# LayerNorm's little tiles allocated in front of the big buffers

## The chip, the cores and the metric

The kernel runs on one core of one Trainium2 chip. The metric is the device time of one execution in microseconds (us): the median of the runs of a kernel.

## The reference

With x of 2048 rows and 512 columns (float32) the kernel computes a gated Fourier mixing layer:

```python
xn  = (x - mean(x)) / sqrt(var(x) + 1e-5)                  # over the 512 columns
a   = xn @ dft_hid_re.T;  b = xn @ dft_hid_im.T
s   = dft_seq_re @ a - dft_seq_im @ b                      # 2048 x 2048 by 2048 x 512
h   = relu(xn @ w1 + b1)                                   # 512 -> 1792
g   = silu((h * h) @ w2 + b2)                              # 1792 -> 512
out = x + s * g
```

## The kernel before

Every float32 operand is kept as a sum of two parts, a high and a low one, of a type that TensorE reads (`F32R`, 4 bytes an element), and each product is three matmuls: high by high, high by low, low by high (`PASSES`). ScalarE makes the high part (L68), VectorE the low one (L71). Many products are made from four blocks with the seven products of Strassen and Winograd (`PRODUCTS`, numbered 1 to 7 in `ORDER`), so that operands stand in tiles of several slots of 256 columns.

A matmul names two operands in the on-chip memory: a stationary one of 128 columns, which a weight load (LDWEIGHTS) brings into the array, and a moving one of 256 or 512 columns, which streams past it. The stages, in the order in which they run:

- **Plain products**, `products` (L330), c = 0 and 1: each is 192 matmuls of 512 columns. Weights: `XC` (xc0 to xc7, the normalised x). Moving: `part`, in g1a and g1b.
- **Products by seven**, `mm` (L277), c = 2 to 7, eight steps j each, so 48 steps of 42 matmuls of 256 columns. Weights: `XC`. Moving: for the products 1, 2 and 3 the buffers g0a and g0b, for 4, 5, 6 and 7 g1a and g1b (`B_SLOT`).
- **Second transform**, `stage2` (L263), 16 times 24 matmuls of 512 columns, laid between the above. Weights: `PQ` (pq00 to pq11). Moving: `WD` (wd0 and wd1).
- **First dense layer**, `hidden` (L517), four chunks c of tokens with seven units p each, 42 matmuls of 256 columns a unit. Weights: `W1[p]`, for p = 0 to 5 in xc2 to xc7, for p = 6 in g0b (slots 0 to 2, 18 matmuls) and g1b (slots 3 to 6, 24 matmuls). Moving: `xT`, in xc0 and xc1 for the even c, in wd0 and wd1 for the odd c (L307).
- **Second dense layer**, `outer` (L571), again four c with seven p of 42 matmuls. Weights: `ready`, in xc4 to xc6. Moving: `W2[p]`, for p = 0 to 4 in xc0, xc1, xc7, xc2 and xc3, for p = 5 and 6 in wd0 and wd1 (`W2_HOME`, L466).

These stages hold 5136 matmuls; 13 more warm TensorE up at the start (L352). The matmuls of a stage stand in one queue in the program's order. Each waits for its operands alone, and the elementwise work and the transfers for the next steps run beside them. The order is written out by hand.

All on-chip buffers are tiles of one pool. A tag's buffer is given its address when the tag is first asked for, one behind the other, each rounded up to 32 bytes. In front stand 1152 bytes of constants and scratch and the small tiles b1s, b2s, eps, stats and stats_t (L81 to L85), up to byte 3552 of a partition. LayerNorm's little tiles are "bn" (48 bytes, three buffers, L117) and "sm" (16 bytes, three buffers, L127). They are first asked for after xc0 to xc7, r, the pq, g0a and g0b have their places, and before g1a, wd0, g1b, wd1, t, e and sx have theirs.

Of the kernel before, what the change touches and what calls it, by code (L numbers as in the profile page):

```python
# [12 lines left out]
P = 128  # L13
# [48 lines left out]
def fnet_gated_kernel(ctx, tc, x, xt, ct, wd, w1, w2, b1, b2, out):  # L62
# [32 lines left out]
    def buf(tag, shape, name, dtype=F32, bufs=1):  # L95
        return pool.tile(shape, dtype, tag=tag, bufs=bufs, name=name)

    def bcast(src, n):
        return bass.AP(tensor=src.tensor, offset=src.offset, ap=[[0, P], [1, n]])

# [13 lines left out]

    def ln_stats(j, hs=slice(0, 2)):
        t = xr[j]
        sm = buf("bn", [P, 12], f"bn{j}_{hs.start}", bufs=3)  # L117
        for h in range(hs.start, hs.stop):
            bn = sm[:, 6 * h:6 * h + 6]
            nc.vector.bn_stats(bn, t[:, h])  # L120
            nc.vector.bn_aggr(stats[:, :, h, j], bn)

    root = {}

    def ln_root(j, hs=slice(0, 2)):
        n = hs.stop - hs.start
        t = root[j] = buf("sm", [P, 4], f"root{j}_{hs.start}", bufs=3)  # L127
        nc.scalar.activation(t[:, 0:n], stats[:, 1, hs, j], AF.Sqrt, bias=eps)

    def ln_rstd(j, hs=slice(0, 2)):  # L130
# [119 lines left out]
    def pq(c, m, dh, src=None):  # L250
        t = PQ[c, m, dh] = buf(f"pq{m}{dh}", [P, 2, 512], f"pq{c}_{m}_{dh}", F32R)
        if src is not None:
            split(t[:, HI], t[:, LO], src)
        return t
# [28 lines left out]
    def load_rows(c, t):  # L283

        flat = rows.rearrange("a b -> (a b)")
        for m in range(2):
            for h in range(2):
                n = m * S + c * TC + h * 256
                nc.sync.dma_start(t[:, 2 * m + 1 - h], bcast(flat[n:n + 256], 256))
        xT["rows"] = t  # L290
# [46 lines left out]
    with tc.manual_schedule(engines=None):  # L337
# [10 lines left out]
        for n, (count, dtype) in enumerate(zip(WARM, (mybir.dt.bfloat16, F32R))):  # L348
            zeros = buf("g0" + "ab"[n], [P, 512], f"zeros{n}", dtype)
            nc.vector.memset(zeros if n == 0 else zeros.bitcast(F32), 0.0)  # L350
            for _ in range(count):
                nc.tensor.matmul(warm, zeros[:, 0:P], zeros, start=True, stop=True)  # L352
        plain_banks(0)
        ln_stats(0, one)
        ln_root(0, one)
        for h, hs in enumerate((one, two)):
            g = plain_parts(0, 0, hs)
            split_hi(*g)
            ln_rstd(0, hs)
            ln_xn(0, h)  # L360
            split_hi(*xc_parts(0, h))
            if h == 0:
                ln_stats(0, two)
                ln_root(0, two)
            split_lo(*g)
            if h == 1:
                ln_stats(1)
                g = plain_parts(0, 1)
                split_hi(*g)
                ln_root(1)  # L370
            split_lo(*xc_parts(0, h))
            products(0, 0, h, True)
        load_c(0, 3)
        load_x(4)
        for j in range(1, NJ):
            ln_rstd(j)
            for h in range(2):
                ln_xn(j, h)
                split_hi(*xc_parts(j, h))
            split_lo(*g)  # L380
            load_c(*order[j + 3])
            if j + 4 < NJ:
                load_x(j + 4)
            split_lo(*xc_parts(j, 0))
            if j + 1 < NJ:
                ln_stats(j + 1)
                ln_root(j + 1)
            xn_lo = split_lo(*xc_parts(j, 1))
            for h in range(2):
                products(0, j, h, j == 1)  # L390
            g = plain_parts(*order[j + 1])
            split_hi(*g)
            if j == 2:
                nc.sync.dma_start(b1s, b1)
                nc.sync.dma_start(b2s, bcast(b2, D))
        split_lo(*g)

    for n, (c, j) in enumerate(order):
# [20 lines left out]
        if j == NJ - 1:  # L419
            for dh in range(2):  # L420
                for m in range(2):
                    t = pq(c, m, dh)
# [216 lines left out]
    for c, j in steps:  # L639
# [21 lines left out]
        if c == NC - 1:  # L661

            if j in (2, 3):
                q = j - 2
                t = buf(f"xc{2 + q}", [P, 3, 4, 256], f"stage{q}")
# [197 lines left out]
def _launch(arrays, out_shape):  # L863
    import numpy as np
    import concourse.bacc as bacc
    from concourse.bass_utils import run_bass_kernel_spmd

    nc = bacc.Bacc("TRN2", target_bir_lowering=False, num_devices=1, dynamic_dma_scratch_size=1024)
    feed, args = {}, []
    for name, v in arrays.items():  # L870
        v = np.ascontiguousarray(v)
        feed[f"in_{name}"] = v
        args.append(nc.dram_tensor(f"in_{name}", v.shape, mybir.dt.from_np(v.dtype), kind="ExternalInput").ap())
    args.append(nc.dram_tensor("out_0", out_shape, F32, kind="ExternalOutput").ap())
    with tile.TileContext(nc, schedule_with_timeline_sim=True) as tc:
        fnet_gated_kernel(tc, *args)
    r = run_bass_kernel_spmd(nc, [feed], core_ids=[0])
    return r.results[0]["out_0"]
# [25 lines left out]
```

## Time and profile before

| | us |
|---|---|
| median of 3 runs (721.21 to 721.50) | 721.28 |
| span of the profiled execution | 719.5 |
| TensorE busy within that span | 706.7 |
| VectorE busy | 584.7 |
| ScalarE busy | 347.6 |

The profile is of one execution. Its span runs from its first to its last instruction; what lies around the span is the 1.8 us by which the median is above it. PE stands for TensorE's matmuls, PEld for its weight loads, DVE for VectorE, ACT for ScalarE. Matmuls follow each other without a gap in most of the span, and each one's recorded duration overlaps the next, so the time that a matmul takes of the span is read from pieces of the chain: the length of a piece by the number of matmuls in it.

### The profile page before, as it was taken

What the parts mean: (1) busy time and instruction counts of PE and PEld (TensorE: products, weight loads), DVE (VectorE), ACT (ScalarE), POOL (GpSimd) and SP (SyncE); (2) the same over time, 40 slices, a digit from 0 to 9 for tenths busy, and PEclk for the clock granted to TensorE, in tenths of its full rate; (3) what the DMA queues carried; (4) which work ended last, traced back from release to release, by engine and by line L of the source; (5) the groups of instructions that cost most, each with busy time, mean ns of one, the idle gap of its engine ahead of it and who ended that gap; (6) DMA issues with size and microseconds to landing.
All of it is one profiled execution on the core that took longest, in us unless ns stands there. A gap on an engine that the chain in (4) does not pass through costs nothing.

```text
span 719.5 us, 12692 instructions
## 1 busy us (share of the span) xinstructions
PE 706.7 (98%) x5149; PEld 665.4 (92%) x5149; DVE 584.7 (81%) x886; ACT 347.6 (48%) x475; POOL 5.2 (1%) x8
## 2 busy tenths in 40 slices
PE   8999999999999999999999999999999999999996
PEld 5778789999999999999998999999999999999996
DVE  7999554679598697797795955999988979989895
ACT  4438233434353544444542424777767764444441
POOL 0000000000000000000000000000000000101000
PEclk9999999999999999999999999999999999999999
DMA  9622540633553653744824669965625995767643
GB/s 325 217 88 89 169 137 16 220 107 128 206 205 132 218 189 122 273 152 139 298 92 147 224 243 337 352 248 205 255 112 188 343 405 196 187 205 199 219 146 111
DMA packets 55018, 141.09 MB, mean 196 GB/s; under 512 B 5040, under 2 KB 21680, under 8 KB 53680
## 3 DMA queue, kind: packets, MB, share of 16 engines
q1 hardware_dynamic: 49840, 124.56, 49.5%
q10 hardware_dynamic: 4032, 14.68, 5.2%
q0 software_dynamic: 1088, 1.05, 1.0%
q8 instruction: 40, 0.66, 0.3%
q14 instruction: 18, 0.15, 0.1%
HBM read 97.00 MB, written 43.27 MB: 195 GB/s over the span
## 4 chain that ended last, share of the span: by engine, by line
PE 83%; DVE 12%; issue 2%; ACT 1%; DMA 1%; DVEq 0%; ACTq 0%; SPq 0%
PE m_b L277 24%; PE yps L263 12%; PE m_b_o L571 10%; PE hps L517 9%; PE hps_b L517 5%; PE m_bb L277 5%; PE m_ba L277 5%; DVE g L71 3%; PE pq_b L330 3%; PE hps_ba L517 3%; DVE xc L71 2%; PE m_bc_o L571 1%; PE m_ba_o L571 1%; PE m_bb_o L571 1%; PE hps_bb L517 1%
## 5 line engine op out<-in xcount | busy, mean ns | idle before, releaser
L277 PE MATMUL m_b<-g,xc 128*128 128x256 f32 x1440 | 181.6, 281 | 0.0
L277 PEld LDWEIGHTS m_b<-g,xc 128*128 128x128 f32 x1440 | 175.7, 189 | 0.5
L71 DVE TENSOR_TENSOR g<-r,g 128x768 fp32r<-128x768 f32 (+2 forms) x65 | 65.5, 1007 | 45.4 <-ACT g L68 45.4
L68 ACT ACTIVATE g<-r 128x768 fp32r<-128x768 f32 (+2 forms) x65 | 57.4, 886 | 88.4 <-PE m_b L277 46.3
L263 PE MATMUL yps<-wd,pq 128*128 128x512 f32 x384 | 94.6, 395 | 0.0
L263 PEld LDWEIGHTS yps<-wd,pq 128*128 128x128 f32 x384 | 70.2, 188 | 15.2
L571 PE MATMUL m_b_o<-w,g 128*128 128x256 f32 x630 | 79.3, 282 | 0.5 <-ACT m_b_o L564 0.5
L571 PEld LDWEIGHTS m_b_o<-w,g 128*128 128x128 f32 x630 | 76.9, 191 | 0.7 <-ACT m_b_o L564 0.7
L71 DVE TENSOR_TENSOR g<-t,g 128x1024 fp32r<-128x1024 f32 x48 | 58.7, 1222 | 12.0 <-ACT g L68 12.0
L330 PE MATMUL pq_b<-g,xc 128*128 128x512 f32 x240 | 64.6, 399 | 2.9 <-DVE g L71 1.7
L517 PE MATMUL hps<-xT,w 128*128 128x256 f32 x504 | 61.9, 281 | 0.0
L517 PEld LDWEIGHTS hps<-xT,w 128*128 128x128 f32 x504 | 60.9, 190 | 0.1
L330 PEld LDWEIGHTS pq_b<-g,xc 128*128 128x128 f32 x240 | 44.1, 188 | 17.0 <-ACT xc L68 2.6
L68 ACT ACTIVATE g<-t 128x1024 fp32r<-128x1024 f32 x48 | 50.3, 1048 | 16.7 <-PE m_ba L277 6.8
L528 ACT ACTIVATE h<-h,b1s 128x512 f32<-128x512 f32 x56 | 37.4, 715 | 18.2 <-DVE h L229 18.2
L68 ACT ACTIVATE g<-hr 128x768 fp32r<-128x768 f32 (+1 forms) x28 | 35.5, 1266 | 21.0 <-DVE hr L196 6.7
L71 DVE TENSOR_TENSOR g<-hr,g 128x768 fp32r<-128x768 f32 (+1 forms) x28 | 41.6, 1485 | 2.2 <-ACT g L68 2.1
L277 PE MATMUL m_bb<-g,xc 128*128 128x256 f32 x288 | 43.3, 282 | 0.0
L277 PE MATMUL m_ba<-g,xc 128*128 128x256 f32 x288 | 42.9, 281 | 0.0
L277 PEld LDWEIGHTS m_bb<-g,xc 128*128 128x128 f32 x288 | 39.3, 189 | 1.8
L277 PEld LDWEIGHTS m_ba<-g,xc 128*128 128x128 f32 x288 | 38.1, 189 | 0.1
L188 DVE TENSOR_TENSOR t<-r 128x512 f32<-128x512 f32 x48 | 32.9, 685 | 5.0 <-DMA r<-in_ct 4.8
(167 smaller groups left out, 1007.7 us busy)
## 6 DMA issues: line engine op xcount, KB each, us to landing
r<-in_ct SPq DMA_DIRECT2D x63, 512.0 KB, 3.5
hd<-h ACTq DMA_DIRECT2D x28, 512.0 KB, 4.6
hr<-hd SPq DMA_DIRECT2D x28, 512.0 KB, 4.7
w1d<-w0g SPq DMA_DIRECT2D x21, 512.0 KB, 3.4
w<-w1d SPq DMA_DIRECT2D x6, 1792.0 KB, 9.3
w<-w2d SPq DMA_DIRECT2D x4, 1792.0 KB, 11.4
y<-ysb SPq DMA_DIRECT2D x16, 256.0 KB, 3.1
fin<-y SPq DMA_DIRECT2D x16, 256.0 KB, 5.1
```

What stands on the lines that cost most here:

```text
L68: nc.scalar.activation(hi, src, AF.Copy)
L71: return nc.vector.tensor_tensor(lo, src, hi.bitcast(F32), op=ALU.subtract)
L188: nc.vector.tensor_tensor(t[:, 0:2], r[:, 0:1].to_broadcast([P, 2, 256]), r[:, 1:3], op=ALU.add)
L263: nc.tensor.matmul(ps, PQ[c, m, k // 2][:, a_, w:w + P], WD[m, k][:, b_, :], start=n == 0, stop=n == 2 * ND * 3 - 1)
L277: nc.tensor.matmul(ps[:, d * CW:(d + 1) * CW], w[:, a_, d * P:(d + 1) * P], mv(b_), start=first and d == 0 and (a_, b_) == (HI, HI), stop= ...
L330: nc.tensor.matmul(accs[c][k], w, g[:, b_, 2 * h:2 * h + 2], start=j == 0 and h == 0 and (a_, b_) == (HI, HI), stop=j == NJ - 1 and h == 1 ...
L517: nc.tensor.matmul(product(ms, k), W1[p][a][:, a_, q * P:(q + 1) * P], xT[c, q][:, b_, b], start=share not in first, stop=q == 1 and (a_, ...
L528: nc.scalar.activation(x_[:, s], x_[:, s], AF.Relu, bias=b1s[:, f:f + 1])
L571: nc.tensor.matmul(m[:, k * 256:(k + 1) * 256], g[:, a_, a, k * P:(k + 1) * P], W2[p][:, b_, b], start=p == 0 and k == 0 and (a_, b_) == ( ...
```

## The change

The three buffers of "bn" and the three of "sm" are allocated at the head of the function, in front of xc0, and the first three uses of each take them from there; later uses ask the pool as before. In the built program every instruction stands where it stood, with the same shapes, waits and signals; the addresses alone differ. The six little tiles take 3 x 64 + 3 x 32 = 288 bytes a partition. So the buffers that stood between byte 3552 and these tiles move up by 288 bytes, and those behind them stay. Start of each buffer, in bytes modulo 256:

| buffers | before | after |
|---|---|---|
| xc0 to xc7 | 224 | 0 |
| the pq (x, pq, fin, rows), r (3 buffers) | 224 | 0 |
| g0a, g0b | 224 | 0 |
| g1a, g1b, wd0, wd1 | 0 | 0 |
| t (2 buffers), e, sx | 0 | 0 |

All slots within these tiles are multiples of 256 bytes long, and a matmul's operand begins at a multiple of 256 bytes from its tile's start, so the table holds for every operand of every matmul.

```diff
+    small = {tag: [buf(tag, [P, n], f"{tag}_{i}", bufs=3) for i in range(3)] for tag, n in (("bn", 12), ("sm", 4))}
+
+    def few(tag, n, name):
+
+        return small[tag].pop(0) if small[tag] else buf(tag, [P, n], name, bufs=3)
...
-        sm = buf("bn", [P, 12], f"bn{j}_{hs.start}", bufs=3)
+        sm = few("bn", 12, f"bn{j}_{hs.start}")
...
-        t = root[j] = buf("sm", [P, 4], f"root{j}_{hs.start}", bufs=3)
+        t = root[j] = few("sm", 4, f"root{j}_{hs.start}")
```

## Rows read from the trace of the kernel before

**Rows 1.** The page, busy time of each engine, and the granted clock in 40 slices.
```profile
PE 706.7 (98%) x5149; PEld 665.4 (92%) x5149; DVE 584.7 (81%) x886; ACT 347.6 (48%) x475; POOL 5.2 (1%) x8
...
PEclk9999999999999999999999999999999999999999
```

**Rows 2.** Waits of PE, whole span: us in total, times, longest us.
```profile
PE pq_b L330 <- DVE g L71: 1.7, 2, 1.3
PE m L571 <- DVE g L71: 1.3, 1, 1.3
PE warm L352 <- DVE zeros L350: 1.2, 1, 1.2
PE pq_b L330 <- ACT xc L68: 0.9, 2, 0.7
PE m_b_o L571 <- ACT m_b_o L564: 0.5, 1, 0.5
```

**Rows 3.** Chain that ended last, 455 to 475.3 us: start, us, what, matmuls.
```profile
455.20 5.04 PE hps L517 x42
460.24 0.72 PE hps_bb L517 x6
460.96 1.43 PE hps_ba L517 x12
462.39 2.83 PE hps_b L517 x24
...
465.22 4.95 PE hps L517 x42
```

**Rows 4.** Windows of those two units: us, PE, PEld, DVE, ACT, POOL, clock, DMA, GB/s.
```profile
455.20:460.24 5.04, 5.04 (x45) 5.04 (x44) 4.76 (x9) 2.85 (x5) 0.00 (x0) 1.00 1.03 409
465.22:470.17 4.95, 4.95 (x45) 4.95 (x44) 3.78 (x7) 3.51 (x6) 0.00 (x0) 1.00 0.76 310
```

**Rows 5.** Tile hps, first 455 to 460 us, then 465.3 to 470: ns minimum/median/maximum.
```profile
L517 PEld LDWEIGHTS hps<-xT,w x42: 192/192/192, 454.9 to 459.8; 128*128 128x128 f32 x42
L517 PE MATMUL hps<-xT,w x42: 283/283/284, 455.0 to 460.0; 128*128 128x256 f32 x42
...
L517 PE MATMUL hps<-xT,w x42: 278/280/284, 465.1 to 469.9; 128*128 128x256 f32 x42
L517 PEld LDWEIGHTS hps<-xT,w x40: 187/188/188, 465.2 to 469.8; 128*128 128x128 f32 x40
```

**Rows 6.** Chain, 494.5 to 503 us: the unit of c = 1 and p = 6.
```profile
494.91 5.00 PE hps L517 x42
```

**Rows 7.** Chain in the second dense layer, 581 to 607 us: p = 2, 5 and 6.
```profile
581.41 3.60 PE m_b_o L571 x30
...
596.53 3.53 PE m_b_o L571 x30
...
601.47 3.53 PE m_b_o L571 x30
```

**Rows 8.** Chain in the products by seven, 144 to 160 us: three steps j.
```profile
144.36 3.56 PE m_b L277 x30
147.92 0.71 PE m_ba L277 x6
148.63 0.71 PE m_bb L277 x6
149.34 3.56 PE m_b L277 x30
...
159.32 0.72 PE m_b L277 x6
```

**Rows 9.** Chain, matmuls of 512 columns: 417 to 437 us, and 80 to 91 us.
```profile
423.84 11.20 PE yps L263 x48
...
83.36 2.10 PE pq_b L330 x9
```

**Rows 10.** Elementwise groups by shape, whole span: xcount | busy us, mean ns.
```profile
L71 DVE TENSOR_TENSOR g<-t,g 128x1024 fp32r<-128x1024 f32 x48 | 58.7, 1222 | 12.0 <-ACT g L68 12.0
L302 DVE TENSOR_TENSOR xr<-xr,rows 128x1024 f32<-128x1024 f32 x12 | 14.7, 1222 | 0.2
```

**Rows 11.** Transfers by line: KB each, median us from issue to landing.
```profile
r<-in_ct SPq DMA_DIRECT2D x63, 512.0 KB, 3.5
w0raw<-in_w SPq DMA_DIRECT2D x7, 512.0 KB, 4.5
```

**Rows 12.** Chain, the longest pieces of the whole span: all of its transfers.
```profile
0.74 2.75 DMA x<-in_x
15.13 3.90 DMA r<-in_ct
```

## The prediction

> **What bounds the kernel now.** I read the page's busy times first: PE is busy for 706.7 of the 719.5 us and runs at the full granted clock, 2.4 GHz, in every slice [rows 1]. Then I read PE's own waits over the whole span: five of them, 1.7 + 1.3 + 1.2 + 0.9 + 0.5 = 5.6 us [rows 2]. So from the end of the start (some 14 us) to the tail (the last 7 us) the time is a count of matmuls times the time that each takes, and only what changes a matmul's time can move the end by much. An edit that moves addresses alone can do that only if operands at other addresses are read at another speed. So the third view is the chain of waits, in order of time, where equal matmuls stand in pieces that can be divided by their number.
>
> **What the pieces show.** In the first dense layer the units of an even c have both operands at 224 modulo 256 (xT in xc0 and xc1, W1 in xc2 to xc7); the units of an odd c have the moving operand at 0 (wd0, wd1) and the weights at 224. The last full unit of c = 0 takes 5.04 us for 42 matmuls, 120.0 ns each; the first of c = 1 takes 4.95 us, 117.9 ns each [rows 3]. The same code ran, 10 us apart, at a granted clock of 1.00 in both windows [rows 4]. In the first every weight load is recorded with 192 ns, in the second with 187 or 188, and the matmul with 283 and 280 ns at the median [rows 5]. I call the first kind a like pair (both starts agree modulo 256) and the second an unlike pair.
>
> That could still be the moving operand's own start (0 better than 224), and then the change would help. The units of p = 6 tell these apart, since 24 of their 42 weights come from g1b, which begins at 0. For c = 1 that makes 24 pairs with both operands at 0 and 18 unlike ones: the unit takes 5.00 us [rows 6], and (5.00 - 18 x 0.1179) / 24 = 119.9 ns, the price of a like pair although both starts are multiples of 256. For c = 0, with the moving operand at 224 and those weights at 0, the last 24 matmuls of p = 6 (18 of them with weights from g1b, unlike) take 2.83 us [rows 3]: (2.83 - 6 x 0.120) / 18 = 117.2 ns, unlike and fast. So all four cases of the two starts are in the trace, and only their agreement counts.
>
> The second dense layer says it a third time: with W2 at 224 (p = 2 here, as for all p to 4) 30 matmuls take 3.60 us, 120.0 ns each; with W2 in wd0 and wd1 (p = 5 and 6), against weights at 224, 3.53 us, 117.7 ns each [rows 7]. In the products by seven the weights are at 224, 18 of a step's 42 matmuls have a moving operand at 224 and 24 at 0. Three steps take 159.32 - 144.36 = 14.96 us, 4.987 us each [rows 8]; 18 x 120.0 + 24 x 117.8 ns gives 4.987.
>
> **The change part by part.** After it every operand of every matmul begins at a multiple of 256, so every pair is a like pair.
>
> Matmuls of 256 columns. Unlike before, like after: 48 steps x 24 = 1152 in the products by seven; in the first dense layer 6 units x 42 x 2 = 504 (c = 1 and 3), their p = 6 with weights from g0b 18 x 2 = 36, and for c = 0 and 2 those with weights from g1b 24 x 2 = 48; in the second one 42 x 2 x 4 = 336 (p = 5 and 6). Together 2076. The price of one is 120.0 - 117.8 = 2.2 ns, so 2076 x 2.2 ns = +4.6 us. Its bounds: 2.0 ns (from the 119.9 of the pairs at 0, against 117.9) gives 4.2 us, 2.33 ns (3.60 - 3.53 us over 30) gives 4.8. The like pairs of before stay at 120.0: both starts move together.
>
> Matmuls of 512 columns. All 768 (L330 and L263) are unlike now: 11.20 us for 48 is 233.3 ns each, and 2.10 us for 9 is the same [rows 9]. The first 24, at the start, stand behind VectorE's work and don't count; 744 remain. No row shows a like pair of this length. From below: the extra time could vanish behind a longer stream, 0. From above: it could grow with the columns, 2 x 2.2 = 4.4 ns, 3.3 us in all. I take 2.2 ns for each, +1.6 us, because there is one weight load of 128 columns for each matmul in either case, and it is the weight load whose record grows by 4 to 5 ns in a like pair [rows 5].
>
> No gap hides these terms: PE's waits in the stretch add up to a few us, and what it waits for there (a split on VectorE, a bias on ScalarE) follows from earlier matmuls, so it moves along.
>
> The two statements that changed cost nothing: the same instructions run with the same waits.
>
> Elementwise work on other addresses. A subtraction of 1024 elements takes 1222 ns with all its operands at 0 (t and g1a or g1b) and 1222 ns with all of them at 224 (xr and rows in the pq buffers) [rows 10]. Zero, and VectorE and ScalarE have slack beside PE.
>
> Transfers. 512 KB from HBM land after 3.5 us in r (at 224) and after 4.5 us in e (at 0) [rows 11]; the load of other transfers differs, but nothing here favours 0. In the chain the transfers hold 2.75 + 3.90 = 6.65 us, all in the first 19 us [rows 12]. Even a tenth off both would be 0.7 us, and for the second, PE is still fed from earlier tiles. I take 0, with -0.5 as the lower bound.
>
> Sum: 4.6 + 1.6 = +6.2 us on the profiled execution, 719.5 to 725.7 us. The median stands 1.8 us above the span, so the forecast is 721.28 + 6.2 = 727.5 us. With all terms at their lower ends, 4.2 + 0 - 0.5 = +3.7 us: 725.0. At their upper ends, 4.8 + 3.3 = +8.1 us: 729.4.
>
> **A rule against it.** The trace gives 120.0 ns where the starts agree and 117.9 where they don't [rows 3]. The Trainium skill, in "SBUF — State Buffer", section "Who interferes with whom", gives TensorE two independent read ports, one for the moving operand and one for weight loads, and says that it never waits for anyone. By that rule the addresses could not matter to a matmul and the two terms would be 0. The trace does not agree with it; the measurement decides.
>
> **The rivals.** *No change.* Then 120.0 against 117.9 ns would come from something else that changes with c and p, such as the traffic: the DMA share was 1.03 in the slow window and 0.76 in the fast one [rows 4], and PE shares the memory with it. The time would be 721.3, within 0.2%. Against it: in p = 6 the price changes within one unit with the weights' buffer, both ways [rows 3, 6], and records of 192 ns without any spread [rows 5] do not look like chance collisions. A gain of the transfers alone (-0.5 us, 720.8) belongs here too. In "DMA: Bandwidth & Descriptors", section "How a descriptor splits into AXI transactions", the Trainium skill has reads that don't start at a multiple of 256 bytes fetch a part in vain, which speaks for the change; an estimate from it for 4096 bytes that begin 32 bytes below a boundary is 135 beats in place of 128. No row here shows that, and transfers hold only the pieces of [rows 12] in the chain.
>
> *Faster.* The moving operand's own start decides: at 0 it is read in 117.8 ns whatever the weights do. Then those matmuls gain that now have both operands at 224, and nothing loses: 864 in the products by seven, 12 units x 42 + 18 x 2 = 540 with c even in the first dense layer, and 5 x 42 x 4 = 840 in the second, in all 2244 x 2.2 ns = -4.9 us: 716.4 us. For it: the two cases with most matmuls fit. Against it: the two small ones don't, 119.9 ns for the pairs at 0 [rows 6] and 117.2 ns for a moving operand at 224 beside weights at 0 [rows 3]. It decides if those two units' times came from something else, and it would show at once in the units of c = 0.
>
> *Slower by more.* The 512-column term grows with the columns: 729.2. It is inside the range.
>
> **How the numbers follow.** The forecast, every pair at the like price, 0.86; its middle is 727.5. No change, with the transfers' gain, 0.08. Faster, 0.06. The forecast's own bounds are 725.0 to 729.4; I let the range begin at 724.5, since the mean price of L277 rests on mixed pieces, and end at 729.6. It leaves out the two rivals, 0.14, and little of the forecast. A measurement of this kernel can tell about 0.2% (1.4 us) from no change, so: faster 0.06, the same 0.08, slower 0.86.
>
> **What would show it.** Right: in the new trace all units of L517 take 5.04 us, those of c = 1 and 3 among them; the pieces of 30 in L571 take 3.60 us for every p; the steps of L277 take 5.04 us in place of 4.99; weight loads of 256-column matmuls are recorded longer than 188 ns; pieces of L263 show 235 to 236 ns a matmul, which settles the term that I could only bound; VectorE's 1222 ns stay. Wrong: units of c = 0 at 4.95 us (the moving operand decides), or the old mix of 5.04 and 4.95 at the old places (traffic or position decides). If the 256-column pieces come out as said and the total doesn't, the 512-column price is what failed.

## The result and the profile after

The changed kernel takes 723.43 us in the median of 8 runs (723.06 to 724.73), against 721.44 us (721.21 to 721.68) for the kernel before in the same runs: a ratio of 1.0030, with a 95% interval of 1.0020 to 1.0041. It is slower, as forecast, but by 2.0 us and not by 6.2, and it lies below the range that was given (724.5 to 729.6). The profiled execution has a span of 721.5 us, 2.0 more than before.

The lines of the new code are six higher: L517 is now L523, L571 is L577, L277 is L283, L263 is L269, L330 is L336. First the page's busy times and granted clock, as in [rows 1]:

```profile
PE 707.4 (98%) x5149; PEld 669.5 (93%) x5149; DVE 584.8 (81%) x886; ACT 347.5 (48%) x475; POOL 5.2 (1%) x8
...
PEclk9999999999999999999999999999999999999998
```

The chain that ended last, in order of time (start, us, what, matmuls), at the start and at the places of [rows 3, 7, 8 and 9]: the first transfer, the end of the plain products, the products by seven, the last blocks of the second transform, the first dense layer with c = 0 and then c = 1, the second dense layer with p = 2 and p = 5, and the last matmuls.

```profile
0.74 2.65 DMA x<-in_x
...
95.29 2.04 PE pq_b L336 x9
...
100.73 5.44 PE yps L269 x24
...
111.61 0.71 PE m_bb L283 x6
...
148.47 3.60 PE m_b L283 x30
...
153.51 3.60 PE m_b L283 x30
...
424.14 10.91 PE yps L269 x48
...
455.20 5.04 PE hps L523 x42
...
462.40 2.88 PE hps_b L523 x24
465.28 5.04 PE hps L523 x42
...
582.74 3.60 PE m_b_o L577 x30
...
597.86 3.60 PE m_b_o L577 x30
...
708.25 2.17 PE m_bb_last L577 x18
```

Every piece of 256-column matmuls is now at 120.0 ns: 5.04 us for 42, 3.60 for 30, 2.88 for 24, wherever it stands. That is the forecast, and these pieces alone would have given it. But the matmuls of 512 columns have become faster: 10.91 us for 48 (227.3 ns) in place of 11.20 (233.3), 5.44 us for 24, 2.04 us for 9 in place of 2.10 [rows 9]. I had forecast the other sign for them.

Waits of PE over the whole span, as in [rows 2]:

```profile
PE pq_b L336 <- DVE g L71: 2.3, 2, 1.9
PE pq_b L336 <- ACT xc L68: 2.0, 3, 1.1
PE m L577 <- DVE g L71: 1.3, 1, 1.3
PE warm L358 <- DVE zeros L356: 1.2, 1, 1.2
PE m_b_o L577 <- ACT m_b_o L570: 0.2, 1, 0.2
```

They sum to 7.0 us, 1.4 more than before, and those of the plain products alone went from 2.6 to 4.3. A part of what the 512-column matmuls save is waited away there.

Five places, at which both executions do the same piece, make a ledger of the 2.0 us. These pieces of the chain of before are new here: three of VectorE's, of which the last ends a wait of PE in the plain products (c = 1), the matmuls behind that wait, the first product by seven and the last matmuls. The piece at 423.84 us is in [rows 9], and its end is the fourth place.

```profile
32.55 0.61 DVE bn L120
...
65.21 3.04 DVE xc L71 x4
...
72.49 1.23 DVE g L71
...
73.77 2.13 PE pq_b L330 x8
...
112.53 0.72 PE m_bb L277 x6
...
706.27 2.15 PE m_bb_last L571 x18
```

Of after, the end of that wait is new, and the other pieces are above:

```profile
72.37 1.22 DVE g L71
...
73.64 2.11 PE pq_b L336 x8
```

| place | before, us | after, us | ahead or behind |
|---|---|---|---|
| plain products, behind the wait | 73.77 | 73.64 | 0.13 ahead |
| first product by seven | 112.53 | 111.61 | 0.92 ahead |
| last two blocks of the second transform | 423.84 | 424.14 | 0.30 behind |
| first dense layer, unit 1 | 423.84 + 11.20 = 435.04 | 424.14 + 10.91 = 435.05 | level |
| last 18 matmuls | 706.27 | 708.25 | 1.98 behind |

At 74 us the lead is 0.13, and 0.10 of it is the first transfer (2.65 us in place of 2.75 [rows 12]): the 267 matmuls of 512 columns before that wait have brought next to nothing. Those from there to 112 us bring 0.79. Between 112 and 424 us the two are 1.22 apart: the products by seven lose 2.6 us (48 steps of 42 at 120.0 ns), and the twelve blocks of the second transform among them give 1.4 back. From 435 us on there are 256-column matmuls alone, and they lose 2.0, as the forecast had it for L517 and L571 (588 + 336 = 924 matmuls by 2.2 ns).

### The profile page after: what moved, and what is told of

It is laid out like the page before. It is cut to its first block, busy times and chain, and to the rows that moved or that the text cites. A ratio compares the mean times of both kernels' runs of the same rounds, so it can differ in the third digit from the quotient of the medians.

```text
span 721.5 us, 12692 instructions
## 1 busy us (share of the span) xinstructions
PE 707.4 (98%) x5149; PEld 669.5 (93%) x5149; DVE 584.8 (81%) x886; ACT 347.5 (48%) x475; POOL 5.2 (1%) x8
## 4 chain that ended last, share of the span: by engine, by line
PE 91%; DVE 6%; ACT 1%; DMA 1%; issue 1%; DVEq 0%; SPq 0%; ACTq 0%
PE m_b L283 24%; PE yps L269 12%; PE m_b_o L577 10%; PE hps L523 10%; PE pq_b L336 6%; PE hps_b L523 6%; PE m_ba L283 5%; PE m_bb L283 5%; PE hps_ba L523 3%; DVE g L71 2%; PE m_bc_o L577 1%; PE hps_bb L523 1%; PE m_bb_o L577 1%; PE m_ba_o L577 1%; PE pq_ba L336 1%; PE pq_bb L336 1%
## 5 line engine op out<-in xcount | busy, mean ns | idle before, releaser
L283 PE MATMUL m_b<-g,xc 128*128 128x256 f32 x1440 | 183.6, 283 | 0.0
L283 PEld LDWEIGHTS m_b<-g,xc 128*128 128x128 f32 x1440 | 177.8, 192 | 0.5
L269 PE MATMUL yps<-wd,pq 128*128 128x512 f32 x384 | 92.6, 390 | 0.0
L269 PEld LDWEIGHTS yps<-wd,pq 128*128 128x128 f32 x384 | 70.4, 188 | 13.3
L577 PE MATMUL m_b_o<-w,g 128*128 128x256 f32 x630 | 79.7, 283 | 0.3 <-ACT m_b_o L570 0.2
L577 PEld LDWEIGHTS m_b_o<-w,g 128*128 128x128 f32 x630 | 77.3, 192 | 0.7 <-ACT m_b_o L570 0.7
L336 PE MATMUL pq_b<-g,xc 128*128 128x512 f32 x240 | 64.2, 396 | 4.5 <-DVE g L71 2.3
L523 PE MATMUL hps<-xT,w 128*128 128x256 f32 x504 | 62.4, 283 | 0.0
L523 PEld LDWEIGHTS hps<-xT,w 128*128 128x128 f32 x504 | 61.4, 192 | 0.1
L336 PEld LDWEIGHTS pq_b<-g,xc 128*128 128x128 f32 x240 | 44.0, 188 | 18.2 <-ACT xc L68 3.6
L283 PE MATMUL m_bb<-g,xc 128*128 128x256 f32 x288 | 43.4, 283 | 0.0
L283 PE MATMUL m_ba<-g,xc 128*128 128x256 f32 x288 | 43.3, 283 | 0.0
L283 PEld LDWEIGHTS m_bb<-g,xc 128*128 128x128 f32 x288 | 39.5, 191 | 1.5
L283 PEld LDWEIGHTS m_ba<-g,xc 128*128 128x128 f32 x288 | 38.5, 192 | 0.1
```

The lines of the kernel that those rows point to most:

```text
L269: nc.tensor.matmul(ps, PQ[c, m, k // 2][:, a_, w:w + P], WD[m, k][:, b_, :], start=n == 0, stop=n == 2 * ND * 3 - 1)
L283: nc.tensor.matmul(ps[:, d * CW:(d + 1) * CW], w[:, a_, d * P:(d + 1) * P], mv(b_), start=first and d == 0 and (a_, b_) == (HI, HI), stop= ...
L336: nc.tensor.matmul(accs[c][k], w, g[:, b_, 2 * h:2 * h + 2], start=j == 0 and h == 0 and (a_, b_) == (HI, HI), stop=j == NJ - 1 and h == 1 ...
L523: nc.tensor.matmul(product(ms, k), W1[p][a][:, a_, q * P:(q + 1) * P], xT[c, q][:, b_, b], start=share not in first, stop=q == 1 and (a_, ...
L577: nc.tensor.matmul(m[:, k * 256:(k + 1) * 256], g[:, a_, a, k * P:(k + 1) * P], W2[p][:, b_, b], start=p == 0 and k == 0 and (a_, b_) == ( ...
```

## Experiments

All kernels but two do the same work with the same instructions, in the same order and with the same waits; only where the buffers begin differs, set by pads and by the order in which the tags are first asked for. The other two measure the price of a pair by itself. Theory going in: the distance between the start of the moving operand and that of its weights, modulo 256 bytes, sets the time of a matmul, and a distance of 0 costs more at 256 columns and less at 512. First rival: what helped the 512-column matmuls is that their operands begin at multiples of 256 bytes.

### All starts at 224: alignment without a multiple

```diff
+    buf("pad", [P, 56], "pad")
     small = {tag: [buf(tag, [P, n], f"{tag}_{i}", bufs=3) for i in range(3)] for tag, n in (("bn", 12), ("sm", 4))}
```

> The changed kernel with 224 more bytes in front, so that every big buffer begins at 224 modulo 256 and none at 0; all pairs of a moving operand and its weights still agree, and no instruction differs. Theory (what counts is whether the two starts agree, and an agreeing pair is dear at 256 columns, 120.0 against 117.8 ns, but cheap at 512, 227.9 against 233.4 ns): the same time as the changed kernel, 723.4 us, 256-column pieces at 120.0 ns and stage2 at 227.9 ns a matmul. Rival (the gain of the 512-column matmuls comes from starts at multiples of 256 bytes): 512-column matmuls back at 233.4 ns, 768 x 5.5 ns = +4.2 us less some 1.5 us of waits that vanish, so 726 us.

Measured: 724.76 us, 1.0045 of the kernel before (1.003 to 1.006). The chain, second transform and second dense layer (L270 and L578 here):

```profile
424.86 10.91 PE yps L270 x48
...
584.71 3.60 PE m_b_o L578 x30
```

10.91 us for 48 matmuls and 3.60 for 30, as in the changed kernel, although no big buffer begins at a multiple of 256. The rival would have put the first at 11.20. So it does not matter that every big buffer begins at a multiple of 256 bytes; that all of them begin at the same place modulo 256 does. The pieces decide this and not the total, which lies between the two forecasts: its median is 1.3 us above the changed kernel's, and the intervals of the two ratios overlap. In the profiled execution a wait of 1.0 us stands that the changed kernel's does not have:

```profile
PE hps_ba L524 <- DMA w1b<-w1d: 1.0, 1, 1.0
```

This is the load of W1 for p = 6. From issue to landing it took 23.2 us here, 20.7 in the kernel before and 20.5 in the changed one, and it is late in two of the other layouts too (below). Whether the addresses or chance make it late, no run here shows.

### The second transform alone

```diff
+    for tag, shape, bufs in (
+        ("xc0", [P, 7, 2, 256], 1),
...
+        ("sm", [P, 4], 3),
+        ("pq00", [P, 2, D], 1),
...
+        ("g1a", [P, 2, 4, CW], 1),
...
+    ):
+        buf(tag, shape, f"at_{tag}", bufs=bufs)
```

(The order is that of before, save that the four pq stand behind "sm".)

> The kernel before with one move alone: the four pq buffers, which hold the weights of the second transform, begin at 0 modulo 256, as its moving operand in wd0 and wd1 does; all other starts modulo 256 and all instructions are those of before. Theory: the 384 matmuls of L263 fall from 233.4 to 227.9 ns, -2.1 us, 719.3 us, everything else as before. Rival (the gain at 512 columns needs the other pairs to agree too, or is lost in waits behind it): 721.4 us.

Measured: 720.08 us, 0.9979 of before (0.9969 to 0.9989): by the ratio -1.5 us for the expected -2.1. The chain (L291 is the second transform, L545 the first dense layer with c = 1):

```profile
422.57 10.90 PE yps L291 x48
...
464.26 4.95 PE hps L545 x42
```

The matmuls of L263 alone fell to 227.1 ns, and the unlike pairs of the first dense layer stayed at 4.95 us for 42. So for the gain at 512 columns its own pair has to agree, and no other. The second transform ends 1.57 us ahead of the kernel before (422.57 + 10.90 = 433.47 against 435.04 us), and the first unit of c = 1 starts 0.96 ahead (464.26 against 465.22 [rows 3]). The 0.6 us between them are lost at two matmuls of c = 0 and p = 6, where PE waits for w1b (the list of waits counts 0.3 us of it).

### Pairs by themselves

```diff
+PHASES = (0, 4, 8, 16, 32, 64, 96, 128, 160, 192, 224, 240, 256, 288, 384, 480, 512, 1024)
+SIZES = (128, 256, 384, 512)
...
+        for n in SIZES:
+            for k, d in enumerate(PHASES):
+                ps = acc.tile([P, 512], F32, tag="abcd"[k % 4], name="p" + "abcdefghijklmnopqr"[k])
+                for i in range(COUNT):
+                    nc.tensor.matmul(ps[:, 0:n], weights[:, i % 4], moving[:, d // 4:d // 4 + n], start=True, stop=True)
```

> Leaves the whole computation out: only matmuls on tiles of zeros, 24 for each of 18 distances (0 to 1024 bytes) between the start of the moving operand and that of the weights and for 128, 256, 384 and 512 columns, with no other engine at work; the output is zeros. Theory: distances that are multiples of 256 bytes (0, 256, 512, 1024) give 120.0 ns at 256 columns and 227.9 at 512, so by the line through these two about 66 ns at 128 and 174 at 384; all other distances give 117.8 and 233.4, so about 60 and 176. Rival (the two prices come from the other engines' and the transfers' traffic to the same memory): without that traffic all distances cost the same at each column count.

This kernel and the next one, of matmuls alone, were each measured in one execution. The chain, 24 matmuls a piece; the letter behind p is the distance in the order of the list (pa 0, pf 64, ph 128, pj 192, pm 256, pr 1024). First 256 columns, then 512:

```profile
60.10 2.93 PE pa L85 x24
...
74.60 2.72 PE pf L85 x24
...
85.87 2.73 PE pj L85 x24
...
94.25 2.88 PE pm L85 x24
...
108.51 2.88 PE pr L85 x24
...
186.85 5.48 PE pa L85 x24
...
214.76 5.50 PE pf L85 x24
...
225.86 5.60 PE ph L85 x24
...
253.88 5.47 PE pm L85 x24
...
281.58 5.44 PE pr L85 x24
```

The mean spacing of the matmuls within each piece, in ns, its first three and its last left out, for some of the distances:

| columns | distance 0, 256, 512, 1024 | 32 | 64 | 96, 128 | 192 | 224, 480 |
|---|---|---|---|---|---|---|
| 128 | 111.7 | 111.7 | 111.6 | 111.6 to 111.8 | 111.6 | 111.6 |
| 256 | 119.7 to 120.1 | 116.6 | 113.3 | 118.5 to 119.8 | 113.3 | 118.3 |
| 384 | 173.3 to 174.5 | 173.4 | 173.3 | 176.0 to 176.5 | 174.9 | 173.4 to 174.1 |
| 512 | 226.7 to 227.2 | 233.2 | 228.7 | 233.2 to 233.8 | 233.3 | 233.4 |

(The piece at 512 columns and distance 0 is the first after a change of length; its mean, 227.8, holds one long gap and is not in the table. Its median spacing is 227 ns.)

The output's transfer lands at 27 us, among the pieces of 128 columns; beside the others no other engine works and the memory traffic is a few GB/s. The slow and the fast price stand here all the same, so the rival that they come from the traffic of others falls. The unlike pairs of the kernel before lie at a distance of 32 (moving operand at 0, weights at 224) or 224: 116.6 and 118.3 ns here, around the kernel's 117.8; at 512 columns all its pairs lie at 32, 233.2 ns here and 233.3 there. The modulus is right: 256, 512 and 1024 bytes act as 0. What I expected wrongly is the rest. The unlike distances are not one class but a landscape, with 113.3 ns at 64 and 192 and 126.6 at 8; the straight line through two lengths fails (128 columns take 111.7 ns at every distance, where I had 60 and 66); and the order of the distances changes with the length. At 256 columns an agreeing pair is among the slow ones, at 512 it is the fastest. What in the chip makes the distance count, no run here shows.

### The fine landscape

```diff
-PHASES = (0, 4, 8, 16, 32, 64, 96, 128, 160, 192, 224, 240, 256, 288, 384, 480, 512, 1024)
-SIZES = (128, 256, 384, 512)
+PHASES = tuple(range(0, 256, 8)) + (256,)
+SIZES = (256, 512)
```

> Leaves the whole computation out, as e2_pairs: matmuls on zeros alone, 24 for each distance from 0 to 256 bytes in steps of 8, at 256 and 512 columns; the output is zeros. Theory (the time depends on the distance modulo 256, and 64 is a broad best for 256 columns): 113 to 114 ns from about 56 to 72 and from 184 to 200, 117 to 120 elsewhere; at 512 columns 227 to 229 at 0, 64 and 256 and 230 to 237 elsewhere. Rival (64 and 192 are single points, of the multiples of 64 alone): neighbours at 56 and 72 cost 117 ns or more.

The chain at 256 columns for the distances 64 (pba) and 192 (pda), then at 512 for 256 (pea):

```profile
34.06 2.83 PE pba L85 x24
...
79.81 2.74 PE pda L85 x24
...
284.71 5.46 PE pea L85 x24
```

There is no broad best: 56 and 72, 184 and 200 cost 118.3 to 120.0 ns. And 64 itself, 113.3 ns in the run before, has a mean of 117.8 here, although the operands lie exactly as they did. Two things differ: what ran just before, and the accumulator that the matmuls write, one of four that take turns over the list of distances. 192 gave 113.6, and 512 columns repeated (228.7 at 64, 227.2 at 256). At 112 bytes the spacing falls to about 113 ns in the last twelve matmuls of the piece. (The distances up to 40 ran beside the output's transfer here, so the 120.0 ns at 8, against 126.6 in the run before, is no clean comparison.) So the distance alone doesn't fix the time of a 256-column matmul: at 64 there are two steady spacings, called rhythms below. That was in neither theory.

### Two layouts built from the landscape

```diff
+    for tag, shape, bufs in (
+        ("bn", [P, 12], 3),
+        ("sm", [P, 4], 3),
+        ("xc2", [P, 7, 2, 256], 1),
+        ("xc3", [P, 7, 2, 256], 1),
+        ("xc7", [P, 7, 2, 256], 1),
+        ("padb", [P, 16], 1),
+        ("g0a", [P, 2, 3, CW], 1),
...
+        ("padc", [P, 16], 1),
+        ("xc4", [P, 7, 2, 256], 1),
...
+        ("padd", [P, 16], 1),
+        ("xc0", [P, 7, 2, 256], 1),
...
```

> The kernel before with the same instructions and other addresses alone: modulo 256, xc2, xc3 and xc7 begin at 0, the g0 and g1 buffers at 64, xc4 to xc6 at 128, and xc0, xc1, wd0, wd1, the pq and all else at 192, so that most pairs of 256 columns lie 64 bytes apart either way (113.3 ns in the run of matmuls alone), the rest 128 (118.5 ns), and the second transform's operands 0 (227.2 ns). Theory (the distance of the two starts modulo 256 sets a matmul's time, and nothing else of the addresses): L277 1512 x 113.3 + 504 x 118.5 ns, 8.0 us less than before; L517 1008 x 113.3 + 168 x 118.5, 5.7 less; L571 672 x 113.3 + 504 x 118.5, 3.6 less; L263 2.0 less; L330 0.3 less: -19.6 us, 701.7 us. Rival (the matmuls become as short, but VectorE, at 78 to 91% beside them, or a transfer ends last): PE's waits grow by the difference, and the time falls by half of it or less, 711 us or more.

Measured: 716.27 us, 0.9921 of before (0.9905 to 0.9938). It is faster than the kernel before, by 5.0 us and not by 19.6. The chain in the first dense layer (L548), for c = 1 the units p = 2 (weights in xc6, distance 64) and p = 4 (weights in xc2, distance 192), then for c = 2 the unit p = 5 (weights in xc3, distance 192):

```profile
473.27 4.95 PE hps L548 x42
...
482.98 4.76 PE hps L548 x42
...
522.22 4.95 PE hps L548 x42
```

4.95 us is the old 117.8 ns, 4.76 us is 113.3. The fast rhythm came for c = 0, 1 and 3 at p = 3 to 5, and for c = 2 it did not, with the same buffers, accumulators and unit before it as for c = 0. For c = 0 the same unit p = 5, from the timeline of PE, takes 456.05 - 451.28 = 4.77 us to the start of the next:

```profile
451.28 4.92 PE L548 MATMUL hps<-xT,w 128*128 128x256 f32 x42
456.05 0.87 PE L548 MATMUL hps_bb<-xT,w1a 128*128 128x256 f32 x6
```

So neither the addresses nor the accumulator fix the rhythm. Nearly everywhere else at 64 or 192, L277 and L571 among it, the spacing stayed at 117.8. That the matmuls did not become as short as expected is most of the miss, so the rival of this run fails too: PE's waits sum to 9.4 us in place of 5.6, which is 3.8 of the 14.6 us that are missing. A transfer has the longest of them:

```profile
PE hps_ba L548 <- DMA w1b<-w1d: 1.9, 1, 1.9
```

The second layout has 192 wherever it can, against agreeing starts for the rest:

```diff
+    for tag, shape, bufs in (
...
+        ("xc2", [P, 7, 2, 256], 1),
...
+        ("xc7", [P, 7, 2, 256], 1),
+        ("padb", [P, 48], 1),
+        ("g0a", [P, 2, 3, CW], 1),
...
+        ("xc0", [P, 7, 2, 256], 1),
...
```

> The kernel before with the same instructions and other addresses alone: modulo 256, xc2 to xc7 begin at 0, and xc0, xc1, the g0 and g1 buffers, wd0, wd1, the pq and all else at 192. The moving operand then lies 192 bytes behind its weights in 1512 matmuls of L277, 1008 of L517 and 672 of L571; the other 1176 of 256 columns and the second transform's have agreeing starts. Theory (a stream of matmuls at such a distance has two rhythms, 117.8 and 113.3 ns, and at 192 it falls into the fast one wherever a run of equal distances is long): 3192 x 113.5 + 1176 x 120 ns, 503.4 us, 14.9 less than before; L263 2.0 less: -17 us, 704 us, less what VectorE and the load of w1b give back. Rival (the rhythm is an accident of what ran just before, and stays at 117.8 ns in L277 and L571 as in the run with 64 bytes): 1176 x 2.2 = 2.6 us more for agreeing pairs than for unlike ones: 4368 x 117.8 + 2.6 = 517.1 us, 1.2 less than before, and with L263 -3 us, 718 us.

Measured: 716.67 us, 0.9941 of before (0.9923 to 0.9959); the profiled execution is at the lower end of the runs, with a span of 714.1 us. The chain in L277 (L306), then in L571 (L600) for p = 4 and p = 5:

```profile
148.77 3.53 PE m_b L306 x30
...
587.76 3.60 PE m_b_o L600 x30
...
592.78 3.40 PE m_b_o L600 x30
```

The fast rhythm (3.40 us for 30, 113.3 ns) now stands in the second dense layer at p = 5, right behind a unit of agreeing pairs, for the first three c, where the layout before had 117.8 at a distance of 64. In L277 and in the first dense layer all 192-byte pairs stayed at 117.8, also those right behind the agreeing pairs of p = 6, so an agreeing unit before it does not start the rhythm by itself. The rival, that the pairs stay at 117.8, is nearer in L277 and L517 and in the total (718 us), the theory in a part of L571. What starts the fast rhythm stays open: distance, what ran before, and the spacing of the parts within a tile differ between the stages that have it and those that don't, but in the first of the two layouts c = 0 and c = 2 agree in all three and differ in the rhythm.

## Why the prediction was wrong

*What bounds the kernel.* Right from 74 us on. Before, it was wrong: the prediction let the count of matmuls begin at "the end of the start (some 14 us)", but the chain of the kernel before runs mostly through pieces of VectorE until the wait that ends at 73.77 us. Of the 744 matmuls that it counted at 512 columns, 243 stand before that wait.

*The price at 256 columns, +4.6 us.* Right in its mechanism, its sign and its size: 120.0 ns in all pieces of after, from L283 to L577. The four cases read out of one trace were enough to tell agreement from the moving operand's own start; the run with all starts at 224 confirms it.

*The price at 512 columns, +1.6 us.* This is the step that failed: "From below: the extra time could vanish behind a longer stream, 0." No row showed an agreeing pair of that length, and the prediction took the sign from 256 columns and let the size alone be open. The weight load's longer record [rows 5], on which I put the price, says little: in the changed kernel's second transform, where the agreeing pairs are fast, the loads are recorded with 188 ns at the median, and with 187 before. Measured: 233.3 to 227.3 ns in the pieces of 48, -6.0 ns where +2.2 was forecast. In the groups by line the busy time of the second transform (before, then after)

```profile
L263 PE MATMUL yps<-wd,pq 128*128 128x512 f32 x384 | 94.6, 395 | 0.0
```

```profile
L269 PE MATMUL yps<-wd,pq 128*128 128x512 f32 x384 | 92.6, 390 | 0.0
```

went from 94.6 to 92.6 us, -2.0 for 384 matmuls. The prediction had named this sign of being wrong: the 256-column pieces came out as said, and the total didn't. A bound from below that allowed the same size with the other sign would have been -3.3 us, and the range would have held the result, but by luck: 744 times 6.0 ns is 4.5 us, of which 2.5 arrived.

*"No gap hides these terms."* Half right. It holds from 74 us on. In the first plain products (c = 0), and in the second up to the wait at 74 us, the gain was waited away, because VectorE sets the pace there. Windows of 14.2 to 58 us (us, PE, PEld, DVE, ACT, POOL, clock, DMA, GB/s), before and then after:

```profile
14.20:58.00 43.80, 43.26 (x182) 33.66 (x183) 42.54 (x92) 18.75 (x33) 0.00 (x0) 1.00 0.48 173
```

```profile
14.20:58.00 43.80, 43.27 (x184) 33.81 (x185) 42.54 (x92) 18.91 (x34) 0.00 (x0) 1.00 0.50 169
```

VectorE is busy for 42.54 of 43.80 us in both (and for all 16.00 us from 58 to 74, in both), and the stretch holds 184 matmuls in place of 182, although 24 of them end to end now take 5.44 us in place of 5.60, so that 4 to 5 more would fit than before. How much of a slower matmul would have counted there, no run shows.

*Transfers and elementwise work, 0.* Right to 0.1 us, as far as the rows tell: the subtraction of 1024 elements in the pq buffers takes 1220 ns in place of 1222, and the two transfers of the chain 2.65 and 3.90 us in place of 2.75 and 3.90 [rows 10, 12].

*The rule against it.* "SBUF — State Buffer" of the Trainium skill, section "Who interferes with whom", gives TensorE two independent read ports. The runs do not agree with what the prediction drew from it: with nothing but PE at work, the distance between the starts of its two operands moves a 256-column matmul from 113.3 to 126.6 ns. Whether the ports are the reason is not shown.

*The sum.* By the ledger: +4.6 us at 256 columns; at 512 columns 0.8 less between 74 and 112 us, 1.4 in the twelve blocks, 0.3 in the last two, -2.5 in all where +1.6 was forecast; and 0.1 less by the first transfer. Together they are the measured +2.0.

## What to carry to other kernels

When matmuls run back to back, look at where the moving operand and the weights begin, modulo 256 bytes, as a pair: the places of the buffers alone were worth -0.8% to +0.45% here. Whether an agreeing pair is good depends on the number of columns, so price each length from its own rows, or by a small run of that length alone; and where no row has the case, leave the sign open as well as the size. And look for the stages in which another engine sets the pace, in the chain and not in the sum of waits: there a faster matmul brings nothing.

## What the runs showed of the hardware

- A matmul's time depends on the distance between the starts of its two operands modulo 256 bytes, without any other engine: in the run of pairs 113.3 to 120.1 ns at 256 columns for multiples of 32 bytes and 126.6 at 8, 226.7 to 234.3 at 512 for multiples of 32. At 128 columns it is 111.6 to 111.8 ns for every distance.
- Agreeing starts are the best at 512 columns (226.7 to 227.2 ns) and among the slowest at 256 (120.0).
- At distances of 64 and 192 bytes a stream of 256-column matmuls has two steady rhythms, 117.8 and 113.3 ns. Which one it takes changed at 64 bytes between two runs of the same pair (with another accumulator), and at 192 between c = 0 and c = 2 of one kernel at the same addresses; what decides is open.
- Whether all starts are at 0 or at 224 modulo 256 makes no difference to PE's pieces (10.91 us for 48 and 3.60 us for 30 in both).
